# Attention, gated MLP and gated convolution in one kernel: the values of attention in column strips of 32, with the first pair's order changed

## The chip, the cores and the metric

The kernel runs on one core of a Trainium2 chip. The metric is the time of one execution on the device, in microseconds (us). The engines are TensorE (PE, with its weight loads listed apart as PEld), VectorE (DVE), ScalarE (ACT), GpSimd (POOL) and SyncE (SP), which issues most of the DMAs here.

## The reference

Three layers follow one another. The change lies in the first.

```python
def _attn_ref(q, k, v, cap):            # (2, 12, 448, 64) each
    scores = np.matmul(q, k.transpose(0, 1, 3, 2)) / np.sqrt(64)
    scores = cap * np.tanh(scores / cap)
    attn = np.exp(scores - np.max(scores, axis=-1, keepdims=True))
    attn = attn / (np.sum(attn, axis=-1, keepdims=True) + 1e-09)
    return np.matmul(attn, v)
...
x = attn_out, heads side by side        # (2, 448, 768)
x = _moe_ref(x, ...)    # x + (u * (w_sg @ norm(v) + b_sg)) @ w_out, u, v = gelu(x @ w_in)
return _moe2_ref(x, ...)  # h = relu(x @ w_in); (h * sigmoid(conv3(h))) @ w_out
```

## The kernel before

Attention works on twelve pairs of heads (six a batch), each in two halves; half 0 is key blocks g = 0 and 1 of 128 keys, half 1 is block 2 and block 3, in which the last 64 keys of both heads share the 128 rows. The loop at the end of `attention` runs over the halves R. For each it issues the scores of half R and, one half later (two from R = 13 on), the values of an earlier half. So PE's row is scores, values, sums, scores, values, sums, with some products of the next layer (`FILL`) between them at five of the halves.

The scores (`sc`) are products of K and Q, each split in a high and a low part, in three terms; the four banks of `sc` are one buffer, so a half's scores wait for the tanh of the half before. ACT takes tanh and exp of them (`raw`). The values (`pv`) multiply `raw`, in plain fp32, with V: of each block the two heads go into partitions 0 to 63 and 64 to 127 of one bank, so the weights are 64 columns wide (128x64); block 3 is one product of full width. The hardware runs an fp32 product as two passes: the trace lists two products and two loads for each instruction. The sums of the exponentials (`su`) are products with ones, 32 columns wide, in four strips of partitions, over half of the 448 columns each (224). In half 0 DVE first adds the two blocks of `raw` (`sm`), so that one group of four strips does.

`ordered` pins each product on PE behind the one before it, so PE's order is the order of the code. DVE, ACT and the queues are put in order by the scheduler of the framework; `lasta` and `lastv` pin some of them. Steps of the decoding of weights (`decode`: the 64-bit words of w_in, conv_w and so on become fp32) are put off by a number of ticks and stand between the steps of attention on DVE and ACT.

At the start PE runs `WARM` products of zeros into a bank of the `su` buffer while the first inputs are loaded (`wps`). In the first pair, whose tanh and exp are done block by block (`soft`), `IDLE` products of zeros follow the scores of each of the blocks 0 and 1 (`idle`). The second half of the first pair (R = 1) passes the values of the first half as `between`: they stand between the scores of block 2 and those of block 3.

Of the kernel before, what the change touches and what calls it, by code (L numbers as in the profile page):

```python
# [9 lines left out]
F32 = mybir.dt.float32  # L10
# [6 lines left out]
P = 128  # L17
B, H, S, D = 2, 12, 448, 64
# [16 lines left out]

TAKEN = 3

WARM = 10

IDLE = 5  # L40

WIN = tuple(0.9 * j for j in range(12))
WOS = (0, 1, 4, 7, 7, 10, 11, 15)
# [5 lines left out]
def stages(  # L49
# [23 lines left out]
    def pin(last):  # L73
        return tc.issue_after(last[0].ins) if last[0] is not None else ExitStack()
# [12 lines left out]
    def f(ap):  # L87
        return ap.bitcast(F32)
# [8 lines left out]
    def mm3(ps, whi, wlo, xhi, xlo, start, stop, matmul=T.matmul):  # L97
        matmul(ps, lhsT=whi, rhs=xhi, start=start, stop=False)  # L98
        matmul(ps, lhsT=whi, rhs=xlo, start=False, stop=False)  # L99
        matmul(ps, lhsT=wlo, rhs=xhi, start=False, stop=stop)  # L100
# [118 lines left out]
    def attention(att, psa):  # L219
# [26 lines left out]
        vf = {}  # L246

        def load_v(n):
            vf[n] = att.tile([P, 4, P], F32, tag="V", name="V", bufs=2)
            nc.sync.dma_start(vf[n], vL[divmod(n, NPAIR)])  # L250
# [25 lines left out]
        load_v(0)  # L276
        if WARM:

            wz = att.tile([P, S], F32R, name="wz")
            V.memset(f(wz), 0.0)  # L280
            wps = psa.tile([P, 512], F32, tag="su", name="wps", bufs=1)[:, :S]
            for i in range(WARM):
                T.matmul(wps, lhsT=wz[:, :P], rhs=wz, start=True, stop=True)
        constants(att)
# [13 lines left out]
        raws, acc, held, pairs = {}, {}, {}, []  # L298
# [3 lines left out]
        def ordered(*args, **kw):  # L302

            with pin(lastm):
                lastm[0] = T.matmul(*args, **kw)  # L305


        def scores(N, half, between=None):

            q, K = Qt[N], Kt[N % 2]  # L310
            ps = psa.tile([P, 4, 512], F32, tag="sc", name="sc", bufs=1)
            raw = raws[N, half] = att.tile([P, 4, S], F32, tag="raw", name="raw", bufs=3)

            sc = {"scale": qscale} if N == 0 else {}

            def soft(t):
                A.activation(raw[:, t], ps[:, t, :S], AF.Tanh, **sc)  # L317
                lasta[0] = A.activation(raw[:, t], raw[:, t], AF.Exp, scale=capc)  # L318

            for g in range(2 * half, 2 * half + 2):  # L320
                c = slice(g * P, (g + 1) * P)
                t = g % 2 * 2
                if g < 3:

                    for i, (j, l) in enumerate(((0, 0), (0, 1), (1, 0))):
                        for h in range(2):
                            r = slice(h * D, (h + 1) * D)
                            ordered(ps[:, t + h, :S], lhsT=K[r, j, c], rhs=q[r, l], start=i == 0, stop=i == 2)
                else:

                    mm3(ps[:, t, :S], K[:, 0, c], K[:, 1, c], q[:, 0], q[:, 1], True, True, ordered)
                if N == 0:
                    soft(slice(t, t + (2 if g < 3 else 1)))
                    for _ in range(IDLE if g < 2 else 0):
                        ordered(idle, lhsT=wz[:, :P], rhs=wz, start=True, stop=True)
                if between and g == 2:
                    between()
            if N:
                soft(slice(0, 4 - half))
            if half == 0:  # L340
                held[N] = att.tile([P, 2, S], F32, tag="sm", name="sm", bufs=2)
                V.tensor_tensor(out=held[N], in0=raw[:, 0:2], in1=raw[:, 2:4], op=ALU.add)

        def values(N, half):
            if half == 0:
                acc[N] = (
                    psa.tile([P, 512], F32, tag="pv", name="pv", bufs=2)[:, :S],
                    psa.tile([P, 512], F32, tag="su", name="su", bufs=1)[:, : S // 2],
                )
            ps, su = acc[N]  # L350
            raw = raws.pop((N, half))
            for g in range(2 * half, 2 * half + 2):
                if g < 3:
                    for h in range(2):
                        r = slice(h * D, (h + 1) * D)
                        ordered(
                            ps[r], lhsT=vf[N][:, g, r], rhs=raw[:, g % 2 * 2 + h],
                            start=g == 0, stop=False, skip_group_check=True,
                        )
                else:  # L360
                    ordered(ps, lhsT=vf[N][:, 3], rhs=raw[:, 2], start=False, stop=True, skip_group_check=True)

            for g in range(2 * half, 3 * half + 1):
                x = raw if half else held.pop(N)
                for t in range(4):
                    h, c = t // 2, (t % 2) * (S // 2)
                    ordered(
                        su[t * 32 : (t + 1) * 32],
                        lhsT=ones[2 if g < 3 else h],
                        rhs=x[:, h if g < 3 else 2, c : c + S // 2],  # L370
                        start=g == 0, stop=g == 3, tile_position=(0, t * 32), skip_group_check=True,
                    )
            if half:
                del acc[N]
                norm(N, ps, su)
# [75 lines left out]
        done = 0  # L451
        for R in range(2 * NN + LAGS[1]):
            N, half = divmod(R, 2)
            if R == 1:
                columns(att)
            for j, at in enumerate(WIN):
                if int(at * 4 + 1) // 2 == R:
                    wdec(*wi_piece(w_in, j // NK, j % NK), att, 4, hi_eng="v", wait=(3, 4, 5))
            if R < 2 * NN:
                if half == 0 and N + 2 < NN:  # L460
                    load(N + 2)
                if R == 1:

                    scores(N, half, lambda: values(0, 0))
                    done += 1
                else:
                    scores(N, half)
                if half == 0 and N + 1 < NN:
                    prep_q(N + 1)
                    prep_k(N + 1)  # L470
            if R in FILL:

                i, k0, k1 = FILL[R]
                if k0 == 0:
                    fill[i] = psm.tile([P, 512], F32, tag="mo", name="mo")[:, :S]
                for k in range(k0, k1):
                    mmw(fill[i], 0, i, k, ordered)
                if k1 == NK:
                    u_done(0, i, fill[i])
            tick()  # L480
            if R - done >= LAGS[R >= LAGS[2]]:
                values(*divmod(done, 2))
                done += 1
            if half and N + 1 < NN:
                load_v(N + 1)
            tick()
# [411 lines left out]
```

## Time and profile before

| what | us |
|---|---|
| median of 3 runs | 342.35 (340.76 to 344.26) |
| the profiled execution, its time | 343.89 |
| the profiled execution, its span | 342.10 |
| PE busy in the span | 329.2 |
| DVE busy | 252.9 |
| ACT busy | 224.9 |
| POOL busy | 35.8 |

The span runs from the first instruction of the trace to the last; the time also holds what lies around it, 1.8 us. The lists below give starts from the beginning of the span. In them the engines overlap; a product's duration in the list contains its way through the array, so that products in a row overlap too, and the distance between starts is what one costs. `x8` counts products as the trace does, two for each fp32 instruction.

### The profile page before, as it was taken

What the parts mean: (1) busy time and instruction counts of PE and PEld (TensorE: products, weight loads), DVE (VectorE), ACT (ScalarE), POOL (GpSimd) and SP (SyncE); (2) the same over time, 40 slices, a digit from 0 to 9 for tenths busy, and PEclk for the clock granted to TensorE, in tenths of its full rate; (3) what the DMA queues carried; (4) which work ended last, traced back from release to release, by engine and by line L of the source; (5) the groups of instructions that cost most, each with busy time, mean ns of one, the idle gap of its engine ahead of it and who ended that gap; (6) DMA issues with size and microseconds to landing.
All of it is one profiled execution on the core that took longest, in us unless ns stands there. A gap on an engine that the chain in (4) does not pass through costs nothing.

```text
span 342.1 us, 5132 instructions
## 1 busy us (share of the span) xinstructions
PE 329.2 (96%) x1814; PEld 252.2 (74%) x1814; DVE 252.9 (74%) x493; ACT 224.9 (66%) x361; POOL 35.8 (10%) x71
## 2 busy tenths in 40 slices
PE   5999999999999999999999999999999999999992
PEld 4544444544456558898899999999999999999991
DVE  3378878889974477997999779997995999970000
ACT  1689988997897246576875554465884988873110
POOL 3000300311034113121111000000000000000000
PEclk9699999999999999999999999999999999999998
DMA  5859555748122114313123383002284113013111
GB/s 174 243 143 278 178 156 158 216 118 218 47 66 63 44 54 148 93 46 94 62 68 119 107 281 150 0 0 62 63 273 158 33 61 92 3 55 126 64 55 34
DMA packets 18698, 37.67 MB, mean 110 GB/s; under 512 B 3980, under 2 KB 9160, under 8 KB 18664
## 3 DMA queue, kind: packets, MB, share of 16 engines
q1 hardware_dynamic: 16952, 34.41, 32.7%
q0 software_dynamic: 1472, 2.61, 2.9%
q8 instruction: 16, 0.26, 0.4%
q10 hardware_dynamic: 240, 0.23, 0.2%
q14 instruction: 18, 0.15, 0.1%
HBM read 34.41 MB, written 2.79 MB: 109 GB/s over the span
## 4 chain that ended last, share of the span: by engine, by line
PE 79%; DMA 7%; DVE 7%; issue 3%; POOL 1%; ACT 0%; SPq 0%; DVEq 0%; ACTq 0%; POOLq 0%
PE mo L98 18%; PE mo L99 17%; PE mo L100 17%; PE pv L305 6%; PE sc L305 5%; PE mo L603 3%; PE mo L604 3%; PE mo L605 3%; PE mo L305 3%; PE su L305 3%; DMA kr<-in_kT_dram 2%; DMA ss<-se 2%; DMA qr<-in_qT_dram 2%; PE idle L305 1%; DVE Q L263 1%
## 5 line engine op out<-in xcount | busy, mean ns | idle before, releaser
L98 PE MATMUL mo<-X,WI 128*128 128x448 f32 x126 | 46.1, 367 | 0.0
L99 PE MATMUL mo<-X,WI 128*128 128x448 f32 x126 | 45.9, 366 | 0.0
L100 PE MATMUL mo<-X,WI 128*128 128x448 f32 x126 | 45.9, 365 | 0.0
L305 PE MATMUL pv<-raw,V 128*64 128x448 f32 (+1 forms) x168 | 43.7, 561 | 0.0
L305 PE MATMUL sc<-Q,K 64*128 64x448 f32 (+1 forms) x252 | 39.7, 398 | 3.4 <-DVE K L92 2.3
L318 ACT ACTIVATE raw<-raw,one 128x1792 f32<-128x1792 f32 (+3 forms) x26 | 39.1, 1503 | 0.6
L305 PEld LDWEIGHTS sc<-Q,K 64*128 64x128 f32 (+1 forms) x252 | 24.8, 190 | 18.0 <-issue 8.1
L130 ACT ACTIVATE f<-f 128x512 f32<-128x512 f32 (+3 forms) x57 | 30.9, 544 | 10.4 <-DMA f<-in_w_out_dram 6.0
L140 DVE SCALAR_TENSOR_TENSOR f<-f 128x512 uint32<-128x512 uint32 (+3 forms) x57 | 30.7, 547 | 9.2 <-ACT f L133 8.7
L317 ACT ACTIVATE raw<-sc 128x1792 f32<-128x1792 f32 (+1 forms) x22 | 32.5, 1475 | 6.8 <-PE sc L305 5.9
L99 PE MATMUL mo<-HG,W 128*128 128x448 f32 x96 | 34.8, 365 | 0.0
L100 PE MATMUL mo<-HG,W 128*128 128x448 f32 x96 | 34.7, 365 | 0.0
L98 PE MATMUL mo<-HG,W 128*128 128x448 f32 x96 | 34.1, 365 | 0.0
L143 DVE SCALAR_TENSOR_TENSOR f<-f 128x512 uint32<-128x512 uint32 (+3 forms) x57 | 30.9, 548 | 0.2
L305 PEld LDWEIGHTS pv<-raw,V 128*64 128x64 f32 (+1 forms) x168 | 11.8, 143 | 21.4 <-issue 18.6
L98 PEld LDWEIGHTS mo<-X,WI 128*128 128x128 f32 x126 | 23.6, 188 | 2.4 <-DVE u L179 0.4
L99 PEld LDWEIGHTS mo<-X,WI 128*128 128x128 f32 x126 | 23.7, 188 | 2.0
L100 PEld LDWEIGHTS mo<-X,WI 128*128 128x128 f32 x126 | 23.6, 188 | 2.0
L783 ACT ACTIVATE o<-mo 128x448 f32<-128x448 f32 x12 | 6.3, 540 | 25.6 <-PE mo L100 22.5
L133 ACT ACTIVATE f<-f 128x256 uint32<-128x256 uint32 (+2 forms) x44 | 22.6, 514 | 0.0
L99 PEld LDWEIGHTS mo<-HG,W 128*128 128x128 f32 x96 | 18.0, 188 | 1.4
L98 PEld LDWEIGHTS mo<-HG,W 128*128 128x128 f32 x96 | 18.0, 188 | 1.4
(141 smaller groups left out, 653.3 us busy)
## 6 DMA issues: line engine op xcount, KB each, us to landing
f<-in_w_in_dram SPq DMA_DIRECT2D x24, 512.0 KB, 4.9
f<-in_w_out_dram SPq DMA_DIRECT2D x24, 256.0 KB, 4.4
V<-in_vL_dram SPq DMA_DIRECT2D x12, 256.0 KB, 4.2
f<-in_w_out_dram SPq DMA_DIRECT2D x8, 384.0 KB, 3.1
qr<-in_qT_dram SPq DMA_DIRECT2D x24, 112.0 KB, 3.2
out_dram<-o SPq DMA_DIRECT2D x12, 224.0 KB, 1.9
rb<-d POOLq DMA_DIRECT2D x22, 112.0 KB, 3.2
kr<-in_kT_dram SPq DMA_DIRECT2D x11, 112.0 KB, 2.6
```

The costliest lines, as they stand in the source:

```text
L98: matmul(ps, lhsT=whi, rhs=xhi, start=start, stop=False)
L99: matmul(ps, lhsT=whi, rhs=xlo, start=False, stop=False)
L100: matmul(ps, lhsT=wlo, rhs=xhi, start=False, stop=stop)
L130: A.activation(f(h), f(h), AF.Copy, scale=2.0**-112)
L133: A.activation(l, l, AF.Copy, scale=0.93 * 2.0**-29)
L140: V.scalar_tensor_tensor(out=l, in0=h, scalar=3, in1=l, op0=ALU.logical_shift_left, op1=ALU.bitwise_or)
L143: V.scalar_tensor_tensor(out=l, in0=h, scalar=0x80000000, in1=l, op0=ALU.bitwise_and, op1=ALU.bitwise_or)
L305: lastm[0] = T.matmul(*args, **kw)
L317: A.activation(raw[:, t], ps[:, t, :S], AF.Tanh, **sc)
L318: lasta[0] = A.activation(raw[:, t], raw[:, t], AF.Exp, scale=capc)
L603: T.matmul(ps, lhsT=xs(0, k), rhs=WI[1][:, 0, k], start=k == 0, stop=False)
L604: T.matmul(ps, lhsT=xs(0, k), rhs=WI[1][:, 1, k], start=False, stop=False)
```

## The change

`value` takes the place of the two kinds of products of the values: for each block, four products of 32 columns each, with the same moving data for the two strips of a head, and for block 3 four strips of its one full-width product. In the first pair, `start_values` and the argument `ahead` put the values of block 0 ahead of the scores of block 2, the values of block 1 ahead of the scores of block 3, and the sums behind the scores of block 3. `WARM` becomes 18, and the zero products go into a bank of the scores' buffer, which is thereby the first to be placed. `IDLE` becomes 4, behind block 0 only.

```diff
-WARM = 10
-
-IDLE = 5
+WARM = 18
+
+IDLE = 4
...
-            wps = psa.tile([P, 512], F32, tag="su", name="wps", bufs=1)[:, :S]
+            wps = psa.tile([P, 4, 512], F32, tag="sc", name="wps", bufs=1)[:, 0, :S]
...
-        def scores(N, half, between=None):
+        def scores(N, half, ahead={}):
...
             for g in range(2 * half, 2 * half + 2):
+                if g in ahead:
+                    ahead[g]()
...
-                    for _ in range(IDLE if g < 2 else 0):
+                    for _ in range(IDLE if g == 0 else 0):
                         ordered(idle, lhsT=wz[:, :P], rhs=wz, start=True, stop=True)
-                if between and g == 2:
-                    between()
...
+        def value(N, g):
+            raw = raws[N, g // 2]
+            for t in range(4):
+                r = slice(t * 32, (t + 1) * 32)
+                ordered(
+                    acc[N][0][r], lhsT=vf[N][:, g, r], rhs=raw[:, g % 2 * 2 + t // 2 if g < 3 else 2],
+                    start=g == 0, stop=g == 3, tile_position=(0, t * 32), skip_group_check=True,
+                )
+
+        def values(N, half, done=False):
+            if not done:
+                if half == 0:
+                    start_values(N)
+                value(N, 2 * half)
+                value(N, 2 * half + 1)
             ps, su = acc[N]
             raw = raws.pop((N, half))
-            for g in range(2 * half, 2 * half + 2):
-                if g < 3:
-                    for h in range(2):
-                        r = slice(h * D, (h + 1) * D)
-                        ordered(
-                            ps[r], lhsT=vf[N][:, g, r], rhs=raw[:, g % 2 * 2 + h],
-                            start=g == 0, stop=False, skip_group_check=True,
-                        )
-                else:
-                    ordered(ps, lhsT=vf[N][:, 3], rhs=raw[:, 2], start=False, stop=True, skip_group_check=True)
...
-                    scores(N, half, lambda: values(0, 0))
+                    start_values(0)
+                    scores(N, half, {2: lambda: value(0, 0), 3: lambda: value(0, 1)})
+                    values(0, 0, True)
```

The first place is the first pair on PE, from the zero products behind the scores of block 0 to the sums of half 0. Rows count instructions here, and what an instruction waits for stands in brackets (DMAHW and DMASW are DMA queues). Before:

```order
L305 MATMUL idle<-wz 128x448 x5
L305 MATMUL sc<-Q,K_87 128x448 [waits Activation_49]
L305 MATMUL sc<-Q,K_87 128x448 x5
L305 MATMUL idle<-wz 128x448 x5
L305 MATMUL sc<-Q,K_87 128x448 [waits Activation_49]
L305 MATMUL sc<-Q,K_87 128x448 x5
L305 MATMUL pv<-raw,V 64x448 [waits DMAHW2_49]
L305 MATMUL pv<-raw,V 64x448
L305 MATMUL pv<-raw,V 64x448 [waits Activation_49]
L305 MATMUL pv<-raw,V 64x448
L305 MATMUL su<-sm,ones_138 32x224 [waits DVE_49,Pool_49]
```

And with the change:

```order
L305 MATMUL idle<-wz 128x448 x4
L305 MATMUL sc<-Q,K_87 128x448 [waits Activation_49]
L305 MATMUL sc<-Q,K_87 128x448 x5
L305 MATMUL pv<-raw,V 32x448 [waits DMAHW2_49,Activation_49]
L305 MATMUL pv<-raw,V 32x448 x3
L305 MATMUL sc<-Q,K_87 128x448 [waits Activation_49]
L305 MATMUL sc<-Q,K_87 128x448 x5
L305 MATMUL pv<-raw,V 32x448 [waits Activation_49]
L305 MATMUL pv<-raw,V 32x448 x3
L305 MATMUL sc<-Q,K_87 128x448 [waits Activation_49]
L305 MATMUL sc<-Q,K_87 128x448 x2
L305 MATMUL su<-sm,ones_146 32x224 [waits DVE_49,Pool_49]
```

The second run of zero products is gone, the values stand in two pieces between the scores of blocks 1, 2 and 3, and the sums stand last.

The second place is a pair in the middle of attention on PE; first its half 0, with the scores ahead of it and behind it:

```order
 L305 MATMUL sc<-Q,K_87 128x448 [waits Activation_49]
 L305 MATMUL sc<-Q,K_87 128x448 x8
-L305 MATMUL pv<-raw,V 64x448 [waits DMAHW1_49,Activation_49]
-L305 MATMUL pv<-raw,V 64x448 x3
-L305 MATMUL su<-sm,ones_138 32x224 [waits DVE_49,PE_49]
-L305 MATMUL su<-sm,ones_138 32x224 x3
+L305 MATMUL pv<-raw,V 32x448 [waits DMAHW1_49,Activation_49]
+L305 MATMUL pv<-raw,V 32x448 x7
+L305 MATMUL su<-sm,ones_146 32x224 [waits DVE_49,PE_49]
+L305 MATMUL su<-sm,ones_146 32x224 x3
```

Then the half 1 that follows, behind the last of these scores:

```order
 L305 MATMUL sc<-Q,K_88 128x448 x11
-L305 MATMUL pv<-raw,V 64x448 [waits Activation_49]
-L305 MATMUL pv<-raw,V 64x448
-L305 MATMUL pv<-raw,V 128x448
-L305 MATMUL su<-raw,ones_138 32x224 x4
-L305 MATMUL su<-raw,ones_136 32x224 x2
-L305 MATMUL su<-raw,ones_137 32x224 x2
+L305 MATMUL pv<-raw,V 32x448 [waits Activation_49]
+L305 MATMUL pv<-raw,V 32x448 x7
+L305 MATMUL su<-raw,ones_146 32x224 x4
+L305 MATMUL su<-raw,ones_144 32x224 x2
+L305 MATMUL su<-raw,ones_145 32x224 x2
```

Nothing moves in either; four instructions of 64 columns become eight of 32, and in half 1 two of 64 and one of 128 become eight.

The third place is DVE at the first pair's sums, with the change; f_164 and f_239 are pieces of w_in, f_202 is conv_w, K and Q those of the third pair.

```order
L95 TENSOR_TENSOR K_88<-kr_90,K_88 128x512 [waits DVE_49]
L135 TENSOR_SCALAR f_164<-f_164 128x512 [waits DMAHW3_49]
L135 TENSOR_SCALAR f_202<-f_202 128x24 [waits DMAHW2_49]
L342 TENSOR_TENSOR sm<-raw 128x896 [waits Activation_49]
L92 CAST K_87<-kr_89 128x512 [waits DMAHW6_49,DMAHW7_49,DMAHW0_49,PE_49]
L262 TENSOR_SCALAR Q<-qr,one 128x448 [waits DMAHW5_49,DMAHW4_49,PE_49]
```

The order is that of the kernel before: the shift of conv_w stands ahead of `sm`, and the third pair's K and Q behind it.

## Rows read from the trace of the kernel before

**Rows 1.** The page: busy time of each engine, and TensorE's granted clock in 40 slices

```profile
PE 329.2 (96%) x1814; PEld 252.2 (74%) x1814; DVE 252.9 (74%) x493; ACT 224.9 (66%) x361; POOL 35.8 (10%) x71
...
PEclk9699999999999999999999999999999999999998
```

**Rows 2.** Timeline of PE, one pair: start us, us, engine, line, operation, count

```profile
23.59 1.69 PE L305 MATMUL sc<-Q,K 64*128 64x448 f32 x9
25.21 1.72 PE L305 MATMUL pv<-raw,V 128*64 128x448 f32 x8
26.86 0.59 PE L305 MATMUL su<-sm,ones 128*32 128x224 f32 x8
27.38 1.49 PE L305 MATMUL sc<-Q,K 64*128 64x448 f32 x12
28.80 1.92 PE L305 MATMUL pv<-raw,V 128*64 128x448 f32 x6
30.65 0.96 PE L305 MATMUL su<-raw,ones 128*32 128x224 f32 x16
31.54 1.68 PE L305 MATMUL sc<-Q,K 64*128 64x448 f32 x9
```

**Rows 3.** Timeline of PE's weight loads (PEld) in the same pair

```profile
25.21 0.20 PEld L305 LDWEIGHTS pv<-raw,V 128*64 128x64 f32 x4 [0.30 <-ACT raw L318]
25.64 0.14 PEld L305 LDWEIGHTS pv<-raw,V 128*64 128x64 f32 x2 [0.23 <-issue]
26.01 0.14 PEld L305 LDWEIGHTS pv<-raw,V 128*64 128x64 f32 x2 [0.23 <-issue]
...
29.70 0.30 PEld L305 LDWEIGHTS pv<-raw,V 128*128 128x128 f32 x2 [0.70 <-issue]
```

**Rows 4.** Timeline of PE at the start; in brackets idle time and what ended it

```profile
1.38 3.86 PE L283 MATMUL wps<-wz 128*128 128x448 f32 x10 [1.38 <-DVE wz L280]
7.55 1.47 PE L305 MATMUL sc<-Q,K 64*128 64x448 f32 x6 [2.31 <-DVE K L92]
8.95 2.23 PE L305 MATMUL idle<-wz 128*128 128x448 f32 x5
11.11 1.49 PE L305 MATMUL sc<-Q,K 64*128 64x448 f32 x6
...
19.43 1.49 PE L305 MATMUL sc<-Q,K 64*128 64x448 f32 x12 [0.72 <-ACT raw L317]
```

**Rows 5.** Stretches: busy us of PE, PEld, DVE, ACT, POOL; granted clock; DMA

```profile
4.82:8.24 3.42, 1.10 (x6) 0.34 (x5) 2.59 (x12) 0.20 (x1) 0.00 (x0) 1.00 0.79 232
8.24:11.65 3.41, 3.37 (x9) 2.28 (x11) 2.41 (x5) 2.05 (x2) 0.00 (x0) 0.50 0.77 239
11.65:15.06 3.41, 3.41 (x13) 2.19 (x11) 0.00 (x0) 2.05 (x2) 0.00 (x0) 0.50 0.93 226
```

**Rows 6.** Timeline of ACT at the start

```profile
9.07 1.01 ACT L317 ACTIVATE raw<-sc,one 128x896 f32<-128x896 f32 x1 [2.26 <-PE sc L305]
10.11 1.04 ACT L318 ACTIVATE raw<-raw,one 128x896 f32<-128x896 f32 x1
...
18.74 0.63 ACT L317 ACTIVATE raw<-sc,one 128x448 f32<-128x448 f32 x1 [0.90 <-PE sc L305]
```

**Rows 7.** Timeline of DVE at the start

```profile
15.06 0.18 DVE L135 TENSOR_SCALAR f<-f 128x24 uint32<-128x24 uint32 x1 [4.34 <-DMA f<-in_conv_w_dram]
15.15 1.09 DVE L342 TENSOR_TENSOR sm<-raw 128x896 f32<-128x896 f32 x1
18.54 0.43 DVE L92 CAST K<-kr 128x512 fp32r<-128x512 f32 x1 [2.30 <-PE sc L305]
```

**Rows 8.** Busy time by stretch, columns as in Rows 5: early pairs, later pairs

```profile
23.59:54.59 31.00, 31.00 (x228) 13.98 (x228) 23.71 (x45) 27.65 (x23) 4.44 (x7) 1.00 0.64 189
54.59:102.57 47.98, 46.71 (x344) 23.21 (x346) 42.86 (x80) 44.58 (x41) 10.32 (x17) 1.00 0.49 137
```

**Rows 9.** Timeline of PE, the longest wait of the later pairs

```profile
78.49 0.59 PE L305 MATMUL su<-sm,ones 128*32 128x224 f32 x8 [0.83 <-DVE se L389]
```

More of the change, by code (lines that the diff above doesn't have):

```diff
@@ L342, in scores, with start_values @@
                 V.tensor_tensor(out=held[N], in0=raw[:, 0:2], in1=raw[:, 2:4], op=ALU.add)
[L344 to L348, printed above, removed]
-                )
+        def start_values(N):
+            acc[N] = (
+                psa.tile([P, 512], F32, tag="pv", name="pv", bufs=2)[:, :S],
+                psa.tile([P, 512], F32, tag="su", name="su", bufs=1)[:, : S // 2],
+            )
[6 more added lines that the diff above has]
+                    start=g == 0, stop=g == 3, tile_position=(0, t * 32), skip_group_check=True,
+                )
+        def values(N, half, done=False):
[4 more added lines that the diff above has]
+                value(N, 2 * half + 1)
             ps, su = acc[N]
             raw = raws.pop((N, half))
-            for g in range(2 * half, 2 * half + 2):
-                if g < 3:
-                    for h in range(2):
-                        r = slice(h * D, (h + 1) * D)
-                        ordered(
-                            ps[r], lhsT=vf[N][:, g, r], rhs=raw[:, g % 2 * 2 + h],
-                            start=g == 0, stop=False, skip_group_check=True,
-                        )
-                else:
-                    ordered(ps, lhsT=vf[N][:, 3], rhs=raw[:, 2], start=False, stop=True, skip_group_check=True)
             for g in range(2 * half, 3 * half + 1):
```

## The prediction

> **What bounds the kernel now.** I read the page first. TensorE (PE) is busy for 329.2 us of a span of 342.1 [rows 1], so the end moves only by what PE loses in work or in waits. The second line of that group shows the granted clock at 6 tenths in the second of the forty slices, against 9 in nearly all others: there is something to win at the start as well.
>
> Next the timeline of PE over one pair of heads in the middle of attention [rows 2]. From the nine score products at 23.59 to the nine of the next pair at 31.54 lie 7.95 us, and each entry begins where the one before it ends; no wait is listed. In these 7.95 us the values (pv) take 1.65 (25.21 to 26.86) and 1.85 (28.80 to 30.65), the sums (su) 0.52 (26.86 to 27.38) and 0.89 (30.65 to 31.54). Eight su products more (16 against 8) cost 0.89 - 0.52 = 0.37 us.
>
> The weight loads of the same pair show the rounds inside these entries [rows 3]. A load for the next round begins when a round of products begins: 25.21, 25.64, 26.01. So the first round of pv takes 0.43, the second 0.37, and the four rounds of 1.65 are 0.43 + 0.37 + 0.37 + 0.48: the last one, ahead of the change from strips of 64 to strips of 32, is 0.10 longer. In the other half two rounds of 64 wide take 29.70 - 28.80 = 0.90, that is 0.43 + 0.47, and the full-width product that follows 30.65 - 29.70 = 0.95, twice 0.475. Every change of width costs about 0.10, at the tail of the round ahead of it. The su rounds have 224 columns: eight products, which are two rounds of four strips, take 0.37, so one takes 0.185, half of 0.37 for 448 columns. Four strips of 32 at once therefore stream as fast as two of 64.
>
> **The values, in strips of 32.** Each half now issues eight 32-wide products, in four rounds of four strips. A half is 0.43 + 3 x 0.375 = 1.55 us, with su behind it in the same width: no drain between them, and the 0.025 by which su's first round is longer today (0.52 is two rounds of 0.187 and some 0.15 around them) goes as well. Half 0 saves 1.65 - 1.55 + 0.025 = 0.13, half 1 saves 1.85 - 1.55 + 0.025 = 0.32, a pair 0.45, the eleven pairs after the first 4.95. The extra products (9 instructions a pair, 108 in all, each of two passes) I cost at nothing: they run beside their neighbours in a round, as su's do. The bound on the other side is 0.06 for each group of four strips (0.43 - 0.37, the only cost at a start that the rows show), 48 groups, 2.9 us. I take zero, since the su rounds are the same form with fewer columns and show zero.
>
> Here a rule speaks against the change. The Trainium skill, TensorEngine Tiling, "Instruction Overhead", gives about 60 cycles for each matmul and warns against tiling a dimension that is already small; for 216 more passes at 2.4 GHz that would be 5.4 us, an estimate from that page, and the steady gain would be gone. The eight su products above, which fit two rounds exactly, do not agree with such a bare cost.
>
> **The start.** Today PE [rows 4] runs ten zero products from 1.38 to 5.24, stands still to 7.55 (until DVE has split K), then come scores at 7.55, five zero products at 8.95, scores at 11.11, five zero products more, scores, pv, su, scores, and only at 19.43 the second pair's scores, which wait for ScalarE (ACT). The granted clock is 1.00 from 4.82 to 8.24, with PE busy for 1.10 of the 3.42 us, then 0.50 for twice 3.41 us, to 15.06 [rows 5]; behind that the slices of [rows 1] stand at 9. Five zero products at 0.50 take 2.16 us (8.95 to 11.11), more than the tanh that follows.
>
> With the change eight more warm-up products stand ahead; at full clock 0.19 each (half of the 0.37 that two passes take), so PE is idle from about 6.75 to 7.55 instead of 5.24 to 7.55, and busy for some 2.6 of the 3.42 us. I take it that the clock then stays; no row shows the activity at which it would, so both ends are kept. The first scores end at 9.0 today, with the clock halved from 8.24; at full clock that is about 8.7. From there ACT sets the pace, with a tanh of 1.01 and an exp of 1.04 for two banks, and a tanh of 0.63 for the last [rows 6]: tanh 8.75, exp 9.8, tanh 10.85, exp 11.9, tanh 12.95, exp 14.0, tanh 15.05 to 15.7. PE fits in between: scores 9.85, pv 10.9 (the exp before it ends at 10.85), scores 11.95, pv 13.0, scores 14.05 to 14.6. The second pair's scores could begin at 15.75.
>
> But su of the first pair stands ahead of them, and it waits for sm on DVE, and in DVE's queue the shift of conv_w stands ahead of sm, in the same order as before. That shift waited 4.34 us for its DMA and ran at 15.06, sm from 15.15 to 16.24 [rows 7]. The queue of SP is not reordered, so I keep 16.24: su 16.3 to 16.8, the second pair's scores at 16.8 instead of 19.43, **2.6 us** earlier. DVE's chain for the next K, Q and the first decoded weights begins when sm and the last scores are done, at 16.24 instead of 18.54, 2.3 earlier; ACT has a small step of conv_w (cw) behind that chain, ahead of the second pair's exp. So the regular pairs begin **2.3 us** earlier. If the clock falls all the same, the same walk with doubled PE entries up to 15 gives su at about 17.0 and the second pair's scores at 18.1, 1.3 earlier; that is the low end. If the clock does not fall in a run of the kernel before, that run has 1.2 of this already.
>
> **What the other engines let through.** The two windows of [rows 8] tell the early pairs from the late. From 23.59 to 54.59 ACT is busy for 27.65 of 31.00, counted with some 0.1 overlap per instruction, and DVE for 23.71: a pair of 7.5 us fits, so its four pairs give 4 x 0.45 = 1.8. From 54.59 to 102.57 ACT has 44.58 of 47.98 and DVE 42.86, and PE already waits 1.27 us there, 0.83 of it at 78.49 for DVE's copy of su [rows 9]. Of the five pairs' 2.25 us I let 0.8 through (about a third; the ends are 0 and all). Behind that come two pairs with the fill products, which give PE more work to a pair than ACT and DVE get by them, so there I take no bound from the two: 0.9. From 122 on nothing is touched; PE has no gap there, and what DVE decodes and what the queues load moves along with it.
>
> Sum: 2.3 + 1.8 + 0.8 + 0.9 = 5.8 us off the profiled execution (span 342.10, time 343.89), which gives 338.1 for it. Its time is 1.5 above the median of the runs; part of that may be the fallen clock, so from the median of 342.35 I take 5.5 instead of 5.8 (a quarter of the 1.2): **336.9 us**. About 1% (3.4 us) is what can be told from no change here.
>
> **The rivals.**
> Everything is kept: ACT's and DVE's stretches shrink with PE's. For: their waits there are waits for each other and for PE. Against: the ACT busy sum above. 2.3 + 4.95 = 7.25, with the same allowance 335.4.
> Later engines take it back: the clock falls all the same (1.3 at the start) and the five middle pairs keep nothing: 1.3 + 1.8 + 0.9 = 4.0, less an allowance of 0.5, 338.9. For: the wait at 78.49, and that the zero products' share needed for the clock is unknown. Here the change does not do what its warm-up is for.
> Each group of strips pays at its start: 2.9 less, 339.8. For: the 0.43 of a first round. The skill's 5.4 above would give 342.3. Against: su's rounds.
> Slower: the four strips take turns at 448 columns because four moving streams are not fed at once. Two rounds of a group become four, 48 x 0.75 = 36 us, about 373. For: no pv row shows four strips at 448. Against: 0.185 against 0.37 scales exactly with the columns. It decides from 5.8 / 48 = 0.12 us a group.
>
> **Chances.** Forecast 0.53 (336.9); all kept 0.17 (335.4); taken back 0.20 (338.9, half on either side of the 1% line at 338.9); cost at each group 0.06 (339.8); turns 0.04 (373). The range takes the first three with a microsecond of spread of a median on either side: 334.3 to 340.2; outside it are the turns and the ends of the others. Faster by over 1%: 0.53 + 0.17 + 0.10 + 0.01 = 0.81; slower 0.04; within 0.15.
>
> **What would show it.** In the changed kernel's timeline: pv x16 in each half taking 1.55 and su straight behind; a pair in 7.5 us; a granted clock of 1.00 from 8.2 to 15; sm at 15.1 with su behind it at 16.3, and scores at 16.8. Wrong would be: pv entries over 1.65; sm much earlier than 15 (then the start gains up to a microsecond more); waits of PE for ACT or DVE between 50 and 100 us that add up to more than 2.7, the present 1.27 and the 1.45 I write off.

## The result, and the profile after

The changed kernel takes 336.88 us in the median of four runs (335.73 to 337.43), the kernel before 342.0 (four runs, 340.76 to 344.26): a ratio of 0.985 [0.9816, 0.9884]. 336.9 was forecast. The profiled execution of the changed kernel took 336.68 us with a span of 334.9, against 343.89 and 342.1; so the two traces lie 7.2 us apart, more than the two medians (5.1), and the walk below is one between traces.

The page of the changed kernel, PE's busy time and the granted clock by slices (before: [rows 1]):

```profile
PE 321.6 (96%) x2032; PEld 251.2 (75%) x2032; DVE 252.6 (75%) x493; ACT 224.3 (67%) x361; POOL 34.9 (10%) x71
...
PEclk9999999999999999999999999999999999999998
```

The 6 in the second slice is gone. PE is 7.6 us less busy with 218 products more in the list: 216 for the 108 added instructions of two passes, eight zero products more at the start and six fewer in `idle`.

PE from the start to the second pair of heads that runs in the steady pattern (before: [rows 4] for the start, [rows 2] for the pair):

```profile
1.38 5.38 PE L283 MATMUL wps<-wz 128*128 128x448 f32 x18 [1.38 <-DVE wz L280]
7.40 1.10 PE L305 MATMUL sc<-Q,K 64*128 64x448 f32 x6 [0.65 <-DVE K L92]
...
9.62 0.88 PE L305 MATMUL sc<-Q,K 64*128 64x448 f32 x6
10.70 0.96 PE L305 MATMUL pv<-raw,V 128*32 128x448 f32 x8 [0.20 <-ACT raw L318]
11.60 0.88 PE L305 MATMUL sc<-Q,K 64*128 64x448 f32 x6
...
13.58 0.88 PE L305 MATMUL sc<-Q,K 128*128 128x448 f32 x3
16.19 0.58 PE L305 MATMUL su<-sm,ones 128*32 128x224 f32 x8 [1.73 <-DVE sm L342]
16.70 1.50 PE L305 MATMUL sc<-Q,K 64*128 64x448 f32 x12
...
22.46 1.71 PE L305 MATMUL pv<-raw,V 128*32 128x448 f32 x16 [0.25 <-ACT raw L318]
23.99 0.56 PE L305 MATMUL su<-sm,ones 128*32 128x224 f32 x8
24.48 1.48 PE L305 MATMUL sc<-Q,K 64*128 64x448 f32 x12
25.89 1.71 PE L305 MATMUL pv<-raw,V 128*32 128x448 f32 x16
27.42 0.94 PE L305 MATMUL su<-raw,ones 128*32 128x224 f32 x16
28.29 1.69 PE L305 MATMUL sc<-Q,K 64*128 64x448 f32 x9
```

Read the starts, not the durations. A half's values take 1.53 us in either half (22.46 to 23.99, 25.89 to 27.42), the sums 0.49 and 0.87, and the following pairs lie 7.49 apart (scores at 28.29, 35.78, 43.27, 50.76), where they lay 7.95 apart. At the start each score product follows a step of ACT, and the long wait has moved: PE now stands 1.73 us at 16.19 for `sm`.

DVE at that point (before: [rows 7]):

```profile
14.87 0.18 DVE L135 TENSOR_SCALAR f<-f 128x24 uint32<-128x24 uint32 x1 [4.40 <-DMA f<-in_conv_w_dram]
14.96 1.08 DVE L342 TENSOR_TENSOR sm<-raw 128x896 f32<-128x896 f32 x1
```

As before, the small shift of conv_w stands ahead of `sm` and waits for its transfer.

Stretches at the start and in the middle (before: [rows 5], [rows 8], with the columns given there):

```profile
4.82:8.24 3.42, 2.77 (x16) 1.98 (x14) 2.83 (x12) 0.20 (x1) 0.00 (x0) 1.00 0.77 238
8.24:11.65 3.41, 3.11 (x22) 1.37 (x20) 2.16 (x5) 3.03 (x4) 0.00 (x0) 1.00 0.76 240
11.65:15.06 3.41, 2.61 (x18) 1.08 (x17) 0.19 (x2) 3.38 (x4) 0.00 (x0) 1.00 0.95 244
...
54.59:102.57 47.98, 46.26 (x434) 25.21 (x435) 41.97 (x76) 45.21 (x41) 11.27 (x20) 1.00 0.40 124
```

The clock stays at 1.00 (2.4 GHz) where it stood at 0.50 (1.2 GHz) for two stretches. In the middle PE is now idle for 1.72 of 47.98 us, against 1.27 [rows 8].

**The lead, stage by stage.** The start of the same entry in the two traces, in us:

| entry | before | after | lead | gained there |
|---|---|---|---|---|
| values, second pair, half 0 | 25.21 | 22.46 | 2.75 | 2.75 |
| the same, sixth pair | 56.99 | 52.41 | 4.58 | 1.83 |
| the same, eleventh pair | 103.32 | 97.07 | 6.25 | 1.67 |
| sums, twelfth pair, half 1 | 121.39 | 114.22 | 7.17 | 0.92 |
| end of the span | 342.1 | 334.9 | 7.2 | 0.0 |

The entries of the second and third line, before:

```profile
56.99 1.72 PE L305 MATMUL pv<-raw,V 128*64 128x448 f32 x8
...
103.32 1.72 PE L305 MATMUL pv<-raw,V 128*64 128x448 f32 x8
```

and after, with PE's waits between them:

```profile
52.41 1.71 PE L305 MATMUL pv<-raw,V 128*32 128x448 f32 x16
...
61.86 1.49 PE L305 MATMUL sc<-Q,K 64*128 64x448 f32 x12 [0.70 <-ACT raw L317]
...
72.66 0.59 PE L305 MATMUL su<-sm,ones 128*32 128x224 f32 x8 [0.23 <-DVE se L394]
73.59 1.70 PE L305 MATMUL sc<-Q,K 64*128 64x448 f32 x9 [0.34 <-ACT raw L317]
...
90.43 1.68 PE L305 MATMUL sc<-Q,K 64*128 64x448 f32 x9 [0.39 <-ACT raw L317]
...
97.07 1.71 PE L305 MATMUL pv<-raw,V 128*32 128x448 f32 x16
```

### The profile page after: what moved, and what is told of

Same layout as the page of the kernel before. It is cut to its first block, busy times and chain, and to the rows that moved or that the text cites. A ratio compares the mean times of both kernels' runs of the same rounds, so it can differ in the third digit from the quotient of the medians.

```text
span 334.9 us, 5570 instructions
## 1 busy us (share of the span) xinstructions
PE 321.6 (96%) x2032; PEld 251.2 (75%) x2032; DVE 252.6 (75%) x493; ACT 224.3 (67%) x361; POOL 34.9 (10%) x71
## 4 chain that ended last, share of the span: by engine, by line
PE 73%; DMA 7%; DVE 6%; issue 6%; ACT 3%; SPq 2%; POOL 1%; DVEq 0%; POOLq 0%; ACTq 0%
PE mo L98 18%; PE mo L99 18%; PE mo L100 18%; PE pv L305 3%; PE mo L610 3%; PE mo L612 3%; PE mo L611 3%; PE mo L305 3%; DMA ss<-se 2%; PE sc L305 2%; DMA f<-in_w_in_dram 2%; DMA kr<-in_kT_dram 2%; DMA d<-ss 1%; POOL rb L421 1%; PE su L305 1%
## 5 line engine op out<-in xcount | busy, mean ns | idle before, releaser
L305 PE MATMUL pv<-raw,V 128*32 128x448 f32 x384 | 41.2, 545 | 0.6 <-ACT raw L318 0.6
L305 PE MATMUL sc<-Q,K 64*128 64x448 f32 (+1 forms) x252 | 38.7, 389 | 2.2 <-ACT raw L317 1.4
L305 PEld LDWEIGHTS pv<-raw,V 128*32 128x32 f32 x384 | 10.0, 109 | 19.8 <-issue 14.7
```

## The experiments

The runs came in four groups: e1 to e4, e5 to e8, e9 to e11, and e12. Each group was timed on one chip beside runs of the kernel before, whose medians there were 342.73, 341.75, 342.37 and 342.82 us. A ratio and its 95% interval are to these runs; they come from all runs and can differ a little from the quotient of the two medians (for e1 0.9882 against 0.9867). Runs of different groups are compared by what each gains on the kernel before, not by their times. Edits are shown against the changed kernel unless it is said otherwise.

### One part alone

`e1_strips_only` has the values in strips of 32 and the old start (zero products and order of the first pair as before; the diff shows the core).

```diff
-WARM = 18
-IDLE = 4
+WARM = 10
+IDLE = 5
...
-                    start_values(0)
-                    scores(N, half, {2: lambda: value(0, 0), 3: lambda: value(0, 1)})
-                    values(0, 0, True)
+                    scores(N, half, {2: lambda: values(0, 0)})
```

> The values in strips of 32 as in the changed kernel; the start (10 warm-up products, 5 and 5 idle products, the first pair's values in one piece, zero products in the su bank) as in the kernel before. If the strips save 0.45 us a pair and the later engines take back what the changed kernel's trace shows (PE's waits between 54 and 103 us grow by 0.6), this run is 4.4 to 4.9 below the kernel before, with pv x16 in 1.53 and a pair in 7.5; the granted clock falls at about 8 as before. If the strips owe their gain to the earlier start (for instance because ACT has no room without it), it is less than 3 below.

Measured 338.18 us, 0.9882 [0.985, 0.9915], 4.55 less than before by the medians and 4.0 by the ratio. The values of a half take 1.53 as in the changed kernel. From the second pair's values to the end it needs 336.0 - 23.74 = 312.3 us where the kernel before needs 342.1 - 25.21 = 316.9: the strips keep 4.6 of their 4.95. In this trace the clock was at 0.50 for one stretch of 3.41 us (8.93 to 12.34), in the trace of before for two [rows 5]. The old start ended 1.47 earlier in it (23.74 against 25.21), but most of that is not the work of the strips. The second pair's scores, which began at 19.43 before [rows 4], begin here at:

```profile
18.27 1.49 PE L305 MATMUL sc<-Q,K 64*128 64x448 f32 x12 [0.72 <-ACT raw L317]
```

So 1.16 us of the lead are there already: K came 0.16 earlier, and one stretch at half clock is missing in this execution, though its warm-up is that of before. Only the last 0.31, from these scores to the second pair's values, go with the first pair's half 1 in strips.

`e2_start_only` has the new start and the values 64 wide.

```diff
-            for t in range(4):
-                r = slice(t * 32, (t + 1) * 32)
...
+            if g == 3:
+                ordered(acc[N][0], lhsT=vf[N][:, 3], rhs=raw[:, 2], start=False, stop=True, skip_group_check=True)
+                return
+            for h in range(2):
+                r = slice(h * D, (h + 1) * D)
```

> The start as in the changed kernel (18 warm-up products, 4 idle, the first pair's values between its scores, sums last), the values 64 wide and block 3 at full width as before. If the two parts add, this run's trace has the second pair's first values at 22.5 to 22.9 and a pair in 7.95 from there; the span is 2.3 to 2.75 below that of the kernel before, the median 1.5 to 2.7 below. If ACT alone sets the pace of the pairs, the lead melts in the middle and less than 1 is left.

Measured 339.76 us, 0.9913 [0.9884, 0.9943], 2.97 less than before, a little over what was expected. All four runs have a mean clock of 0.995. Its pairs take 7.95 again.

`e5_changed_again` is the changed kernel, unchanged, beside the runs of the second group.

> The changed kernel again, to stand beside the three below on the same chip. Ratio 0.985 as before, and the granted clock at 0.995 or more in every run, if its 18 warm-up products and the short stretches without products at the start hold the clock.

Measured 337.05 us, 0.9866 [0.9847, 0.9885]: 4.7 less than before, against 5.1 in the first comparison. The parts alone add up to 4.55 + 2.97 = 7.5. So together they give 2.4 to 2.8 less than their sum; by the ratios it is 4.0 + 3.0 against 5.1 and 4.6, 1.9 to 2.4 less. Each of these gains is known to about 1 us, so that something is lost is likely, but how much is not settled.

### The clock at the start

`e3_warm10` takes the eight warm-up products away again and keeps the new order (`WARM = 10`).

> The changed kernel with 10 warm-up products instead of 18. My theory: the granted clock falls at about 8.2 to 0.50, su of the first pair starts at about 17.0, the second pair's scores at 18.1 instead of 16.7, and the run is 1.2 to 1.4 slower than the changed kernel, about 338.1. Rival: the wait for conv_w's DMA and sm sets the second pair's scores whatever the clock, and the run is within 0.4 of the changed kernel.

Measured 338.31 us, 0.9862 [0.9834, 0.989], with runs from 337.38 to 340.81. That is 4.4 less than before by the medians and 4.7 by the ratio; the changed kernel gained 5.1 and 4.6 by its two ratios. So the expected loss of 1.2 to 1.4 is not shown, and the rival (within 0.4) stands. Stretches of the profiled execution, the slowest of the five (340.81), at the start and at 76 us:

```profile
8.22:11.64 3.42, 3.42 (x12) 2.14 (x12) 2.07 (x5) 2.06 (x2) 0.00 (x0) 0.50 0.80 256
11.64:15.05 3.41, 3.00 (x27) 0.86 (x23) 0.80 (x3) 3.03 (x4) 0.00 (x0) 1.00 0.88 260
...
76.49:79.90 3.41, 3.41 (x12) 2.61 (x13) 3.38 (x8) 0.71 (x1) 0.00 (x0) 0.50 0.95 222
```

And the entry of PE that ended its idle time just ahead of the last of them:

```profile
75.84 0.58 PE L305 MATMUL su<-sm,ones 128*32 128x224 f32 x8 [2.58 <-DVE se L394]
```

The clock did fall without the eight products more, but it came back after one stretch, and the second pair's scores began at 16.60, no later than in the changed kernel; its values began 0.7 later (23.15 against 22.46), held by ACT. The larger loss of this execution came in the middle, where PE stood 2.58 us and the clock fell once more. Nor does the fall come each time: two of the five runs have a mean clock of 0.997, as high as the changed kernel's.

`e4_before_warm18` is the kernel before with `WARM = 18` and nothing else.

> The kernel before with 18 warm-up products instead of 10, nothing else. My theory: the clock stays at 1.00 from 4.8 on, the second pair's scores start at about 18.2 instead of 19.4, and the run is 1.2 below the kernel before, so about half of the start's gain is the clock. Rival: the five and five idle products and the values in one piece still set the pace, the gain is under 0.4.

Measured 342.57 us over ten runs (341.46 to 345.14), 1.0 [0.9964, 1.0035]. The expected gain did not come. PE in the profiled execution, the slowest of the ten (345.14):

```profile
12.74 1.72 PE L305 MATMUL pv<-raw,V 128*64 128x448 f32 x8
16.72 0.59 PE L305 MATMUL su<-sm,ones 128*32 128x224 f32 x8 [2.26 <-DVE sm L342]
...
18.84 2.61 PE L305 MATMUL sc<-Q,K 64*128 64x448 f32 x12 [0.72 <-ACT raw L317]
21.38 3.55 PE L305 MATMUL pv<-raw,V 128*64 128x448 f32 x6
```

and its stretches there:

```profile
14.68:18.09 3.41, 1.37 (x11) 0.67 (x11) 1.31 (x3) 0.26 (x1) 0.00 (x0) 1.00 1.06 307
18.09:21.50 3.41, 2.69 (x15) 1.96 (x16) 3.41 (x8) 2.02 (x5) 0.00 (x0) 0.50 0.69 175
21.50:24.92 3.42, 3.42 (x10) 0.73 (x14) 1.63 (x6) 1.76 (x2) 0.00 (x0) 0.50 0.41 111
```

The clock stood at 1.00 to 18.09, PE was done with the first values at 14.46, stood for `sm` (which stands behind conv_w, and the shift of conv_w ran at 15.40), and then the clock fell for 6.83 us, with the second pair's products in it at twice their time. So the products of zeros bought nothing by themselves: in this execution what they won at the head was waited away at `sm`, and the clock was lost behind that wait. With the new order, the scores of block 3 are done before the wait, and the second pair's scores follow the sums directly. The new order without the eight products was run with the strips only, and there it shows no gain either: e3 is 4.4 less than before (4.7 by the ratio), the strips with the old start (e1, in the same group) 4.55 (4.0). So which part of e2's 2.97 the products and which the order brings is not shown.

`e7_noidle` takes the four zero products behind block 0 away (`IDLE = 0`).

> The changed kernel without the four idle products behind the first scores. If the remaining products keep the clock, nothing moves by more than 0.3, since ACT's tanh sets the next scores. If the four are needed, the granted clock falls to 0.50 at about 11.7 or 15 and the run is 1 to 3 slower.

Measured 335.86 us, 0.9832 [0.9809, 0.9856], against 337.05 of the changed kernel beside it; their intervals overlap. The clock stayed at 1.00 over the start. The four products are not needed; that leaving them out gains is not shown.

### What the strips save

`e8_block3_full` computes block 3 as one product of full width again, all else as in the changed kernel.

```diff
         def value(N, g):
             raw = raws[N, g // 2]
+            if g == 3:
+                ordered(acc[N][0], lhsT=vf[N][:, 3], rhs=raw[:, 2], start=False, stop=True, skip_group_check=True)
+                return
```

> The changed kernel with block 3 as one product of full width again, between strips of 32. My theory (what is saved is the 0.10 at each change of width): half 0 keeps its gain, half 1 takes 1.85 again, a pair is 7.8 instead of 7.5 and the run is 2.5 to 3.5 above the changed kernel. Rival (strips of 32 are faster in themselves, or what counts is the first pair's order): half 1 keeps at least half of its gain and the run is less than 1.5 above.

Measured 339.07 us, 0.9911 [0.9893, 0.9928], 2.0 more than the changed kernel beside it (1.5 by the ratios): less than the 2.5 to 3.5 expected, and not below the rival's 1.5. The trace decides between the two. PE over one pair:

```profile
30.13 1.71 PE L305 MATMUL pv<-raw,V 128*32 128x448 f32 x16
31.66 0.56 PE L305 MATMUL su<-sm,ones 128*32 128x224 f32 x8
...
33.57 1.91 PE L305 MATMUL pv<-raw,V 128*32 128x448 f32 x10
35.40 0.94 PE L305 MATMUL su<-raw,ones 128*32 128x224 f32 x13
```

and the weight loads of its values:

```profile
30.13 0.16 PEld L305 LDWEIGHTS pv<-raw,V 128*32 128x32 f32 x8 [0.31 <-ACT raw L318]
30.53 0.13 PEld L305 LDWEIGHTS pv<-raw,V 128*32 128x32 f32 x4 [0.25 <-issue]
30.91 0.13 PEld L305 LDWEIGHTS pv<-raw,V 128*32 128x32 f32 x4 [0.25 <-issue]
31.29 0.13 PEld L305 LDWEIGHTS su<-sm,ones 128*32 128x32 f32 x4 [0.25 <-issue]
...
34.45 0.30 PEld L305 LDWEIGHTS pv<-raw,V 128*128 128x128 f32 x2 [0.73 <-issue]
```

Half 0, all strips, takes 1.53; half 1, with 32-wide strips and then full width, takes 1.83 (33.57 to 35.40). Its strips run to 34.45, 0.88 for two rounds that take 0.40 + 0.38 in half 0, and the product of full width 0.95 for two passes: 0.30 us in all for the one piece of another form. Of eleven pairs' 3.3 us, 2.0 show in the time; the rest is not taken apart. The loads tell how the strips run: 0.40 from the first round to the second and 0.38 to the third, with no cost at the second group's start at 30.91. The rival that put 0.06 on each group is refuted, and so is the one in which four strips take turns (0.75 a round). The bare cost of an instruction that the Trainium skill, TensorEngine Tiling, "Instruction Overhead", gives (about 60 cycles) is not seen either: 216 passes more went with a shorter half (1.53 against 1.65 and 1.85 [rows 2]).

### A still earlier start, and the middle

`e6_conv_late` puts the steps of conv_w's decoding off by three ticks, so that `sm` need not wait behind them.

```diff
-        decode(cw[:, 0], cw[:, 1], conv_w, pool, 4 if bounded else 3)
+        decode(cw[:, 0], cw[:, 1], conv_w, pool, 4 if bounded else 3, wait=(4, 5, 6) if bounded else (1, 2, 3))
```

> The changed kernel with the three steps of decoding conv_w put off by three ticks, so that the sum sm of the first pair no longer stands behind the shift that waits for conv_w's DMA. My theory (that wait, not the clock or ACT, sets the second pair's scores): sm at 12.7 instead of 14.9, scores of the second pair at 15.2 instead of 16.7, its first values 1 to 1.8 earlier, the run 0.8 to 1.8 below the changed kernel. Rival: the DMA queue, busy at 0.95 until 19, holds what comes next (K and Q of the following pairs, V, the pieces of w_in), the lead is gone by the third pair and the run is within 0.4 of the changed kernel.

Measured 335.76 us (six runs, 334.6 to 337.02), 0.9818 [0.9792, 0.9843], 1.3 less than the changed kernel beside it. The two intervals just miss each other (0.9843 and 0.9847), but the runs overlap, and so does the interval of the first comparison (0.9816 to 0.9884): a gain of about 1 us is likely and not settled. In its trace `sm` ran at 12.90, the second pair's values began at 20.90 (21.71 in the changed kernel beside it), but the sixth pair was level with it again, and the span is 334.5 against 334.4.

`e9_columns_late` loads and decodes conv_w and the norm's gains ten pairs later (`if R == 1:` ahead of `columns(att)` becomes `if R == 21:`); `e10_columns_late_noidle` leaves out the four idle products as well; `e11_columns_late_win`, on top of e10, loads w_in's pieces at a closer distance (`0.9 * j` becomes `0.75 * j` in `WIN`).

> The changed kernel with conv_w and g_ln loaded, and conv_w decoded, at half R = 21 instead of 1, so that neither stands in the queues nor between the steps of the first pairs. If the lead of the run with conv_w put off was lost only because its small step then stood ahead of the third pair's tanh on ACT (0.40) and because the DMA queue was full, the lead of 0.8 to 1.5 at the second pair now lasts: ratio 0.981 or lower, span 333 or lower. If the later pairs are bound by ACT and DVE whatever comes before, the waits of PE between 50 and 100 us grow by the lead and the ratio stays at 0.985 to 0.987.

> The same without the four idle products behind the first scores. As that alone left the clock at 1.00 and the time where it was or below, I expect the same as with them within 0.5; if a shorter start leaves the clock with too few products, it falls at about 12 or 15 and the run is over 1 slower.

> The same as the run before it, with the twelve pieces of w_in spaced at 0.75 pairs instead of 0.9, so that their decoding leaves the stretch in which ACT and DVE have the least room (pairs 6 to 9) sooner. If the work of ACT and DVE in that stretch is what PE waits for there (1.6 to 1.8 us in the changed kernel), the waits shrink by at least 0.6 and the run is 0.5 to 1.5 below the one before it. If the order in which the steps stand is what PE waits for, or the early pairs have no room, it is the same or slower.

Measured: e9 336.25 us, 0.9815 [0.9783, 0.9848]; e10 336.62 us, 0.982 [0.9785, 0.9855], with runs from 335.45 to 339.1; e11 338.27 us, 0.9881 [0.9839, 0.9924]. All three begin the second pair's values at 20.7, 1.0 to 1.8 earlier than the changed kernel (21.71 in e5, 22.46). By the ratios e9 and e10 are 1.0 to 1.8 us better than the changed kernel in its two comparisons, with intervals that overlap; e9 lies just above the 0.981 expected if the lead lasted, and its span is 335.0 and not 333. e11, which was to gain 0.5 to 1.5 on e10, lost 1.65. PE's waits in the trace of e9, between the pairs where it still led (sixth pair at 50.68 against 51.67 in e5) and the end of attention:

```profile
71.69 0.59 PE L305 MATMUL su<-sm,ones 128*32 128x224 f32 x8 [0.98 <-DVE se L394]
...
98.96 1.69 PE L305 MATMUL sc<-Q,K 64*128 64x448 f32 x9 [0.75 <-ACT raw L317]
```

With 0.70 at 60.12, 0.48 at 81.05 and 0.39 at 89.48 they add up to 3.3 us; in the changed kernel, in the same pairs, the waits come to 1.7 (1.8 in e5). In e11 PE stood 3.67 us for `sm` at 56.24, with the clock at 0.50 behind it (56.63 to 60.04); just before, at 51.98, DVE had stood 4.01 us for a transfer into `ss`, of which the next lines tell. In e10 one wait for `se` took 2.51 us, and the clock fell as well:

```profile
74.12:77.53 3.41, 3.41 (x13) 2.60 (x10) 3.38 (x8) 1.19 (x1) 0.00 (x0) 0.50 0.77 177
```

DVE in e10 shows what the copy `se` was late for:

```profile
64.43 0.23 DVE L411 TENSOR_SCALAR ss<-ss,one 128x14 f32<-128x14 f32 x1 [3.08 <-DMA ss<-se]
...
72.76 0.38 DVE L394 COPY se<-su 128x224 f32<-128x224 f32 x1
```

In the normalisation of the sums, POOL issues a small transfer (`ss<-se`), DVE waits for it at the head of its queue, and all that DVE has behind (K, Q, the decoding, then the copy `se` that frees the bank of the next `su`) moves back by as much. Six traces fit one line: DVE's wait for `ss` near 63 us and PE's wait at the `su` that follows are 0.80 and 0.23 (changed kernel), 0.89 and 0.31 (e5), 1.01 and 0.42 (e6), 1.59 and 0.98 (e9), 3.08 and 2.51 (e10), 3.15 and 2.58 (e3), a difference of 0.57 to 0.61 each time. Where DVE's wait there was shorter than that (0.24 in e1, none in e7), PE had no wait for `se`. With block 3 at full width the difference is larger: 1.95 and 0.83 (before), 1.29 and 0.18 (e2), 1.72 and 0.82 (e8). The transfer took 4.2 us from its issue to its landing in the changed kernel and 6.1 in e10; the median of the six of a run is 2.4 and 2.9.

`e12_ss_later` moves the steps that wait for `ss` two ticks back, on top of e9.

```diff
-            later(3, s1)
-            later(4, s1b)
+            later(3 if last else 5, s1)
+            later(4 if last else 6, s1b)
```

> The run with conv_w and g_ln loaded late (four idle products), with the first step of the normalisation (the small addition on ss, which waits for a DMA that gathers the sums) and the DMAs behind it put off by two ticks for all pairs but the last of those. My theory: in the later pairs that addition stands at the head of DVE's queue until its DMA has landed (0.6 to 3.1 us in the traces of these runs), DVE's copy of su comes late by as much, and PE waits for it, in the worst runs long enough for the clock to fall at 56 to 77. Then DVE's waits for ss fall under 0.5 in total, PE's waits for se under 0.4, no run has a fallen clock in the middle, and the ratio is 0.979 or lower, span 333.5 or lower. Rival: DVE and ACT are simply full there; then the waits move to other instructions, add up to the same 3.5 and the ratio stays at 0.9815.

Measured 337.88 us, 0.9871 [0.9837, 0.9906], no better than e9. DVE's waits for `ss` fell to 0.7 us over attention (3.9 in e9), but the next transfer of the chain took their place. DVE and PE:

```profile
66.26 1.09 DVE L428 TENSOR_TENSOR E<-E,rb 128x896 f32<-128x896 f32 x1 [2.10 <-DMA rb<-d]
```

```profile
72.16 0.59 PE L305 MATMUL su<-sm,ones 128*32 128x224 f32 x8 [1.37 <-DVE se L394]
```

DVE waited three times for `rb`, 5.4 us in all, since that transfer starts later by as much as the step ahead of it. That `ss` alone holds up the middle has fallen. The chain of two transfers with fixed places in DVE's queue fits, but is not shown: PE's waits between 50 and 105 us add up to 3.2 us here and to 3.3 in e9, as the rival expected (DVE and ACT simply full there, the waits move to other instructions), and no run decides between the two.

## Why the prediction was right, step by step

**The strips: right.** A half was to take 1.55 and took 1.53; a pair 7.5, and it took 7.49; the four pairs behind the start 1.8, and they gave 1.83. The zero for the extra products, and the extra time where the width changes as the source of the gain, are shown by e8; that this part of the gain lies in the strips is shown by e1 (312.3 against 316.9 us behind the start). One reading behind it was too simple: 0.10 for every change of width accounts for the longer round ahead of the full-width product (0.88 against 0.78), but that product's own 0.95 is 0.20 above two passes of 0.375, and only one change follows it. What makes up the other 0.10 is open; the sum held because it took the two halves as wholes.

**The start: the walk right, the clock's worth not shown, the size short.** The walk had scores at 9.85, 11.95 and 14.05, `sm` at 15.15, su at 16.3 and the second pair's scores at 16.8; they stand at 9.62, 11.60, 13.58, 14.96, 16.19 and 16.70. The term was 2.3 and measured 2.75. Of the 0.45 some 0.2 is that K and conv_w came 0.15 and 0.19 earlier in that execution; the rest is not taken apart. The clock stayed at 1.00, as forecast, but its worth was not what the walk had: for the case that the clock falls, it put the second pair's scores at 18.1, and in e3, where it fell for 3.41 us, they began at 16.60, no later than in the changed kernel, where PE stands 1.73 us for `sm` ahead of them (e3 has no such wait, and conv_w came 0.32 earlier in it). The term also stands against one execution of the kernel before, with two stretches at half clock. That is not every execution's: the mean clock of the 13 runs of before in the first group goes from 0.982 to 0.998, that of the changed kernel's runs from 0.994 to 0.998.

**The middle: the term that was mis-sized.** 0.8 of 2.25 was let through, and 1.67 came through. The argument was ACT's busy sum and the wait for DVE. PE's waits for ACT did grow, from 0.32 us (one) to 1.43 (0.70, 0.34 and 0.39), but the wait for `se` fell from 0.83 [rows 9] to 0.23, along with DVE's wait for `ss` ahead of it, before:

```profile
69.74 0.23 DVE L406 TENSOR_SCALAR ss<-ss,one 128x14 f32<-128x14 f32 x1 [1.95 <-DMA ss<-se]
```

and after:

```profile
63.90 0.23 DVE L411 TENSOR_SCALAR ss<-ss,one 128x14 f32<-128x14 f32 x1 [0.80 <-DMA ss<-se]
```

That wait is another in each execution, so this part of the gain is luck as much as the change. In sum PE's idle time grew from 1.27 to 1.72, by 0.45 and not by the 1.45 that I wrote off.

**The allowance: also off, the other way.** 0.3 was taken off the sum because the profiled execution of before lay above its median. It should have been more: the traces differ by 7.2 us, the medians by 5.1 here and by 4.7 beside e5. So the median came out within 0.1 us since a sum of 5.8 that was 1.4 too small for its own execution met a median that was 1.9 below that execution. That the number is so close is luck: two errors that cancelled.

**Where the rest of the sum goes.** The strips alone give 4.55 and the start alone 2.97, together 4.7 to 5.1. The traces have the same shortfall: 6.1 (e1) and 3.8 (e2) off the span of 342.1, 9.9 in all, against 7.2 and 7.7 (e5). The second pair's values begin at 25.21 before, at 23.74 with the strips alone, at 21.90 with the new start alone, and at 22.46 and 21.71 with both: leads of 1.47 and 3.31 make 4.78, and both together have 2.75 and 3.50. So 1.3 to 2.0 are missing at the start and 0.7 to 0.9 behind it. But both parts are measured against the same execution of before, whose time was 1.9 above the median, and adding them counts that excess once too often. Of e1's 1.47, 1.16 are the earlier K and the stretch at half clock that this execution did not have, and not the strips. Without them 0.1 to 0.9 is missing at the start, and there the wait for `sm` differs by 0.6 between two executions of the same kernel (1.73, and 1.10 in e5). And e2 needs 0.5 less from there to the end than before (316.4 against 316.9), where its wait for `se` was 0.18 and not 0.83. So these traces do not show that the two parts take from each other. By the medians the new start adds 0.2 to 0.6 to the strips and by the ratios 0.5 to 1.1, against 3.0 alone; why it is less stays open. The way from there to the end, in the executions in which the clock didn't fall there:

| run | second pair's values | end | between |
|---|---|---|---|
| e1 | 23.74 | 336.0 | 312.3 |
| changed | 22.46 | 334.9 | 312.4 |
| e7 | 21.76 | 334.2 | 312.4 |
| e5 | 21.71 | 334.4 | 312.7 |
| e6 | 20.90 | 334.5 | 313.6 |
| e12 | 20.80 | 335.5 | 314.7 |
| e9 | 20.70 | 335.0 | 314.3 |

In these executions a lead down to about 21.7 is kept; of what lies beyond, the waits for DVE's `se` and ACT's `raw` take back most. This fits e6 and e9, whose gain on the changed kernel is small and not settled, and e12, which shows none. These are single executions; the medians can't be taken apart so.

**The rivals.** The cost at each group and the turns are refuted by e8. That the clock falls all the same did not happen in any trace of the changed kernel at the start. That everything is kept would have been 7.25, which is what the two traces show (7.2); the medians, 5.1 and again 4.7 in e5, do not bear it out.

**What stays open.** Why the transfer of `ss`, about 7 KB, takes 1.7 us at one time and 6.1 at another was not tried. Whether e6, e7 and e9 beat the changed kernel is not settled; the lowest medians, 335.76 (e6) and 335.86 (e7), were not tried together. Whether the chain of `ss` and `rb` or the plain load of DVE and ACT sets the waits in the middle is open, and so is why the two parts together give less than their sum.

## What to carry to other kernels

Where PE runs without a gap, look in the timeline for changes of form between neighbours: here a round ahead of one took about 0.10 us longer, and giving neighbours the same strips took that away at no price for the extra instructions. A warm-up is worth at most what the next wait lets through (in e4 nothing that could be measured): find what PE will wait for once it is early (here `sm`, behind a small transfer's step in DVE's queue) before paying for it. And where a lead grows, look at what the neighbours have room for: here a lead at the second pair's values was kept down to about 21.7 us, and of a larger one most came back as waits. The gains of two edits on one engine's row need not add: here 7.5 alone and 4.7 to 5.1 together, each known to about 1 us.

## What the runs showed of the hardware that was not expected

After a fall the granted clock stood at 0.50 for 3.41 us at the start of e1 and e3 and in the middle of e3, e10 and e11, and for twice that in the trace of before [rows 5] and in e4. The same program had it and had it not: the ten runs of e4 have mean clocks from 0.984 to 0.998 and times from 345.14 to 341.46, and 3.41 us at half clock are 3.41 / 2 / 343 = 0.005 of such a mean.

A stand of PE cost more than itself where the clock fell behind it: the 2.26 us of e4 were followed by 6.83 us at 0.50, the 2.58 of e3, the 2.51 of e10 and the 3.67 of e11 by 3.41, while the 1.73 us for `sm` in the changed kernel were followed by none.
